# Low halves of eight weight pieces, the first block's sum and the first token mix made on TensorE, in a new order of steps

## The chip, the cores and the metric

The kernel runs on one core of a Trainium2 chip. The metric is the device time of one execution in microseconds (us); smaller is better. The kernel before takes 435.28 us (median of 3 runs, 435.2 to 435.55).

## What is computed

For 4 batches, 8 heads, 768 tokens and heads of 48 channels, a recurrence with a decaying state gives `x`, and a mixing network follows it:

```python
for t in range(S):
    y[:, :, t] = einsum('bhd,bhde->bhe', rt, state + (u * kt) vt)
    state = wt[..., None] * state + kt vt
x = y as (batch, seq, 384)
xt = x.transpose(0, 2, 1)
h = xt @ U @ V                      # U (768, 32), V (32, 768): a mix over tokens
u = x + h.transpose(0, 2, 1)
out = u + relu(u @ w_ch1) @ w_ch2   # 384 -> 1536 -> 384
```

`U`, `V`, `w_ch1` and `w_ch2` come as 64-bit floats, passed as pairs of 32-bit words.

## The kernel before, in words

**Chunks.** The recurrence is cut into 24 chunks of 128 tokens (6 for each batch; functions in `chunk(g)`). For a chunk VectorE makes two scans of the decays (step F, `scan_f`, and Q, `scan_q`; R between them takes reciprocals), and r and k are scaled by them (RP, KS: VectorE or GpSimd, "Pool"). TensorE makes scores (AM, `scores`), VectorE merges them under a mask into A (CP, `merge`), TensorE makes the output (YA from A and v, YZ from the state Z). The state goes from chunk to chunk: KT and KN turn k, DS multiplies it with v, ZM decays the sum (VectorE or ScalarE). The diagonal of A is a sum over channels of r, k and u: PR multiplies r and k, MD sums on TensorE (`rows_by_u`), DV copies, SEL and SEL2 spread it; chunks from 6 on use RK, RU and RED instead. XE brings the output to x (tile `xT`), XT and XN (or XD on VectorE) turn it for the token mix.

**Token mix and blocks.** `token_mix(b)` sums the six chunks of a batch against U (GA twice, G4, SELM; the high and low halves of the result by GS and GSL). The tokens are cut into 7 blocks of 384 or 512. For a block `make_u` multiplies the mix with V into PSUM (HP), adds it to x on VectorE (UADD), and splits the sum in a high half (UH) and a low half (UL), for each of three channel tiles. `ffn` then makes 12 groups UP of nine products each (high and low half of weights and of u), with relu halves HH and HL, and 12 groups DN of nine, the sum O and the store OUT. So block 0 can start only when all six chunks of batch 0 are through.

**Weights.** 27 pieces are loaded raw (LRAW) and converted (`split_raw`): E on ScalarE, C2 and C3 on VectorE (lines 302 and 315), ADD on GpSimd (line 322), the high half HI on ScalarE (line 332), and the low half SUB = value minus high half, on GpSimd or VectorE (line 339).

**Order.** Nothing is scheduled by a tool at build time: the table `ORDER` names each step in turn, three characters a step (its number, and whether it goes to its other engine, and how many warm-up products TensorE runs ahead of it, `lead`). Each engine runs its steps in the order of the table; SP issues all loads and stores in that order too. `plan` gives the buffers out in the same order: 3 PSUM buffers ("ffn") serve UP, DN, HP, XT, KT, MD and the mix; two buffers hold w, so the load LW of a chunk waits for Q of the chunk two before.

## Time and profile before

| | before |
|---|---|
| median of 3 runs | 435.28 us (435.2 to 435.55) |
| the profiled execution: span from first to last instruction | 433.5 us |
| around the span (median less span) | 1.8 us |
| TensorE busy, share of the span | 418.0 us, 96% |
| VectorE busy | 351.0 us, 81% |
| ScalarE, GpSimd busy | 185.5 us, 134.3 us |
| first product of a block (UP) | at 59.46 us |
| last product ends | at 427.97 us |

PE is TensorE, DVE VectorE, ACT ScalarE, POOL GpSimd, SPq the queue that issues the DMAs. A row of a timeline has the start in us, the duration, engine, line of the kernel, operation, the tile written and the tiles read, and how many equal instructions it merges. Products on TensorE overlap, so a row's cost to those behind it is the distance from its start to the next start. A matrix product on plain 32-bit floats shows two records each.

### The profile page before, as it was taken

What the parts mean: (1) busy time and instruction counts of PE and PEld (TensorE: products, weight loads), DVE (VectorE), ACT (ScalarE), POOL (GpSimd) and SP (SyncE); (2) the same over time, 40 slices, a digit from 0 to 9 for tenths busy, and PEclk for the clock granted to TensorE, in tenths of its full rate; (3) what the DMA queues carried; (4) which work ended last, traced back from release to release, by engine and by line L of the source; (5) the groups of instructions that cost most, each with busy time, mean ns of one, the idle gap of its engine ahead of it and who ended that gap; (6) DMA issues with size and microseconds to landing.
All of it is one profiled execution on the core that took longest, in us unless ns stands there. A gap on an engine that the chain in (4) does not pass through costs nothing. (4 is left out here: it accounts for less than half of the span.)

```text
span 433.5 us, 10486 instructions
## 1 busy us (share of the span) xinstructions
PE 418.0 (96%) x4156; PEld 363.0 (84%) x4156; DVE 351.0 (81%) x802; ACT 185.5 (43%) x527; POOL 134.3 (31%) x178
## 2 busy tenths in 40 slices
...
GB/s 279 327 267 338 204 132 310 110 198 172 272 80 217 123 242 158 23 26 107 98 64 231 119 23 117 81 119 122 8 30 74 1 162 39 36 104 206 2 2 60
DMA packets 23913, 57.29 MB, mean 132 GB/s; under 512 B 2864, under 2 KB 7856, under 8 KB 23856
## 3 DMA queue, kind: packets, MB, share of 16 engines
...
q8 instruction: 34, 0.56, 0.5%
...
## 5 line engine op out<-in xcount | busy, mean ns | idle before, releaser
L898 PE MATMUL f<-hid,w2h 128*128 128x384 f32 (+1 forms) x504 | 148.5, 364 | 0.0
L864 PE MATMUL f<-u,w1h 128*128 128x384 f32 (+1 forms) x504 | 147.8, 364 | 0.6 <-DVE xT L820 0.3
L864 PEld LDWEIGHTS f<-u,w1h 128*128 128x128 f32 x504 | 92.9, 188 | 12.9 <-issue 1.4
L898 PEld LDWEIGHTS f<-hid,w2h 128*128 128x128 f32 x504 | 92.9, 188 | 10.2 <-issue 0.7
L864 PE MATMUL f<-u,w1l 128*128 128x384 f32 (+1 forms) x252 | 90.8, 360 | 0.0
L898 PE MATMUL f<-hid,w2l 128*128 128x384 f32 (+1 forms) x252 | 90.7, 360 | 0.0
L869 ACT ACTIVATE hid<-f 128x384 fp32r<-128x384 f32 (+1 forms) x60 | 32.2, 538 | 96.9 <-PE f L864 88.9
L875 DVE SCALAR_TENSOR_TENSOR hid<-f,hid 128x384 fp32r<-128x384 f32 (+1 forms) x84 | 50.0, 608 | 11.2 <-ACT hid L869 10.5
L898 PEld LDWEIGHTS f<-hid,w2l 128*128 128x128 f32 x252 | 47.4, 188 | 4.7
L864 PEld LDWEIGHTS f<-u,w1l 128*128 128x128 f32 x252 | 47.4, 188 | 4.0
L679 DVE STREAM_TRANSPOSE kn<-rk 32x128 f32<-32x128 f32 x160 | 48.3, 302 | 2.5
L469 ACT ACTIVATE A<-ident,dv 128x128 f32<-128x128 f32 x140 | 43.8, 391 | 6.0 <-DVE dv L455 4.0
L916 DVE TENSOR_TENSOR xT<-f,xT 128x384 f32<-128x384 f32 (+1 forms) x21 | 12.7, 610 | 38.0 <-PE f L898 37.9
L831 POOL TENSOR_TENSOR u<-xT,u 128x512 fp32r<-128x512 f32 (+1 forms) x10 | 12.3, 1238 | 91.5 <-PE f L864 35.8
L322 POOL TENSOR_TENSOR cva_w<-cva_w,raw_w 128x384 int32<-128x384 int32 x24 | 25.0, 1055 | 41.1 <-DVE cva_w L315 15.7
L405 DVE TENSOR_TENSOR_SCAN Q<-w,starts,qd 128x258 f32<-128x258 f32 x48 | 33.3, 735 | 0.5 <-POOL rk L413 0.2
L551 DVE COPY_PREDICATED A<-maskf,aps 128x1024 f32<-128x1024 uint32 x24 | 31.6, 1315 | 0.4 <-PE aps L544 0.2
L390 DVE TENSOR_TENSOR_SCAN F<-w,qd 128x259 f32<-128x259 f32 x48 | 30.4, 675 | 0.5 <-DMA w<-in_wT 0.4
L716 DVE STREAM_TRANSPOSE xn<-xT 32x192 f32<-32x192 f32 x80 | 29.5, 369 | 1.1
L413 POOL TENSOR_TENSOR rk<-rk,Q 128x512 f32<-128x512 f32 x18 | 21.5, 1193 | 25.4 <-DVE Q L405 25.4
L871 DVE TENSOR_SCALAR hid<-f 128x384 fp32r<-128x384 f32 (+1 forms) x24 | 14.3, 596 | 17.7 <-PE f L864 14.4
L475 POOL TENSOR_SCALAR_AFFINE_SELECT A<-dv 128x128 f32<-128x128 f32 (+1 forms) x39 | 11.7, 333 | 43.1 <-DVE dv L455 20.0
...
## 6 DMA issues: line engine op xcount, KB each, us to landing
...
```

The source lines that it names most:

```text
L322: lambda: nc.gpsimd.tensor_tensor(out=d["to"].bitcast(I32), in0=d["a"].bitcast(I32), in1=d["e"], op=ALU.add),
L390: nc.vector.tensor_tensor_scan(out=back(F), data0=back(st["w"]), data1=back(qd, OVER * h), initial=1.0, op0=ALU.mult, op1=ALU.add)
L405: nc.vector.tensor_tensor_scan(out=st["Q"][:, a:e], data0=st["w"][:, a:e], data1=qd[:, a - OVER * h : e - OVER * h], initial=starts[:, h : ...
L413: ENG[eng].tensor_tensor(out=rk[:, 0], in0=rk[:, 0], in1=Qv, op=ALU.mult)
L469: nc.scalar.activation(to, one, AF.Copy, scale=dv[:, NP * i + j : NP * i + j + 1])
L551: nc.vector.copy_predicated(to, mask2, new)
L679: nc.vector.transpose(to[32 * j : 32 * j + 32, :, 32 * i : 32 * i + 32], src[32 * i : 32 * i + 32, :, 32 * j : 32 * j + 32])
L716: nc.vector.transpose(to[q, :, :, r], src[r, :, :, q])
L864: nc.tensor.matmul(ps, wt[:, f, ct, :], u[ct][:, z], start=(m == 0), stop=(m == 8))
L869: nc.scalar.activation(h[:, 0], d["ps", f], AF.Relu)
L875: nc.vector.scalar_tensor_tensor(out=h[:, 1], in0=d["ps", f], scalar=0.0, in1=h[:, 0].bitcast(F32), op0=ALU.max, op1=ALU.subtract)
L898: nc.tensor.matmul(d["o", ct], wt[:, 4 * ct + part, f - 3 * part, :], hid[f][:, z], start=(part == 0 and m == 0), stop=(part == 3 and m == 8),
```

## The change

With the lists `LOW_PE`, `X_PE`, `MIX_AT_ONCE` and `UP_PARTS`, and a new table:

- For w1 pieces 0 to 7 the SUB is replaced: TensorE adds the value times the identity and the high half times minus the identity in PSUM (LP, new lines 349 and 350), and ScalarE or VectorE copies the result out (LC). Six of the LC stand on ScalarE, two (w12, w15) on VectorE; a PSUM buffer is held meanwhile.
- Block 0: TensorE brings x into PSUM by the identity (XI) and adds HP to it there; UH and UL read the sum from PSUM, and ScalarE copies it back to x (UC). The three UADD go.
- Batch 0's mix: six steps GX sum one chunk each into one PSUM tile, in place of GA, G4 and SELM.
- UP of f = 0, 1, 2 in block 0 is cut into three steps UA by channel tile (the same nine products in another order).
- MD takes four products of 32 columns in place of one of 128.
- The order of all steps is new, as are the engines of those with two, and the warm-up products (14 before, 28 after).

First place, TensorE early on: MD 2 (`trd_267`), scores of chunk 1, YA 0, MD 3 (`trd_349`) and DS 0 before,

```order
L496 MATMUL trd_267<-u_diag,kr_225 128x2 x4
L544 MATMUL aps<-rk_175 64x128 x4
L544 MATMUL aps<-rk_175 64x64 x4
L544 MATMUL aps<-rk_175 64x128 x4
L544 MATMUL aps<-rk_175 64x64 x4
L622 MATMUL y_325<-A_195,v_193 32x128 x8
L632 MATMUL y_325<-A_195,v_193 32x128 x8
L496 MATMUL trd_349<-u_diag,kr_310 128x2 x4
L561 MATMUL dS<-v_193,kn_320 48x48 x8
```

and after the change (`trd_412` is MD 3, with the last of 9 warm-up products ahead of it, `lp_w` are LP w12 and LP w11):

```order
L200 MATMUL trd_412<-blank 128x384
L522 MATMUL trd_412<-u_diag,kr_408 32x2 x16
L572 MATMUL aps<-rk_214 64x128 x4
L572 MATMUL aps<-rk_214 64x64 x4
L572 MATMUL aps<-rk_214 64x128 x4
L572 MATMUL aps<-rk_214 64x64 x4
L349 MATMUL lp_w_480<-cva_w_2_282,ident 128x384
L350 MATMUL lp_w_480<-w1h,minus 128x384
L349 MATMUL lp_w_489<-cva_w_1_182,ident 128x384
L350 MATMUL lp_w_489<-w1h,minus 128x384
```

The scores of chunk 1 (AM 1) moved from ahead of MD 3 to behind it, and two LP stand behind them.

Second place, TensorE from the block's mix (HP) to the first product of block 0, before (`trk_1070` is KT 7, `trx_0_1114` XT 1.0),

```order
L815 MATMUL hp_2_1062<-Vst,gs_1003 128x384
L522 MATMUL trk_1070<-ident,rk_657 128x128 x4
L561 MATMUL dS<-v_930,kn_1022 48x48 x8
L544 MATMUL aps<-rk_657 64x128 x4
L544 MATMUL aps<-rk_657 64x64 x4
L544 MATMUL aps<-rk_657 64x128 x4
L544 MATMUL aps<-rk_657 64x64 x4
L735 MATMUL trx_0_1114<-ident,xT_1091 128x128 x3
L864 MATMUL f_0_3_1128<-u_0_1039,w1h 128x384
```

and after (YA 6 and HP 0.0 stand just ahead of these rows):

```order
L883 MATMUL hp_1_1180<-xT_438,ident 128x384
L865 MATMUL hp_1_1180<-Vst,gs_1113 128x384
L883 MATMUL hp_2_1186<-xT_438,ident 128x384
L865 MATMUL hp_2_1186<-Vst,gs_1113 128x384
L572 MATMUL aps<-rk_984 64x128 x4
L572 MATMUL aps<-rk_984 64x64 x4
L572 MATMUL aps<-rk_984 64x128 x4
L572 MATMUL aps<-rk_984 64x64 x4
L550 MATMUL trk_1220<-ident,rk_984 128x128 x4
L349 MATMUL lp_w_1225<-cva_w_7_1077,ident 128x384
L350 MATMUL lp_w_1225<-w1h,minus 128x384
L940 MATMUL f_0_3_1246<-u_0_1171,w1h 128x384
```

The two XI and LP w17 are new ahead of the first product; DS 6 went forward out of this stretch, and XT 1.0 behind the first eight groups.

Third place, VectorE from the merge of chunk 6 to the low halves of block 0, before (`gs` is GSL 0; the adds into `xT_436` are UADD),

```order
L551 COPY_PREDICATED A_921<-maskf,aps 128x1024
L781 TENSOR_TENSOR gs_1003<-gb_999,gs_1003 32x384
L390 SCALAR_TENSOR_TENSOR F_1014<-w_957,qd 128x259 x2
L820 TENSOR_TENSOR xT_436<-hp_0_1025,xT_436 128x384
L820 TENSOR_TENSOR xT_436<-hp_1_1037,xT_436 128x384
L820 TENSOR_TENSOR xT_436<-hp_2_1062,xT_436 128x384
L831 TENSOR_TENSOR u_0_1039<-xT_436,u_0_1039 128x384
```

and after:

```order
L579 COPY_PREDICATED A_967<-maskf,aps 128x1024
L809 TENSOR_TENSOR gs_1113<-gb_986,gs_1113 32x384
L479 TENSOR_REDUCE dv_1116<-kr_1052 128x8
L363 TENSOR_TENSOR w1l<-cva_w_8_1055,w1h 128x384
L308 TENSOR_SCALAR cva_w_9_1131<-raw_w_9_1127 128x384
L308 TENSOR_SCALAR cva_w_6_1133<-raw_w_6_1123 128x384
L321 SCALAR_TENSOR_TENSOR cva_w_9_1131<-raw_w_9_1127,cva_w_9_1131 128x384
L321 SCALAR_TENSOR_TENSOR cva_w_6_1133<-raw_w_6_1123,cva_w_6_1133 128x384
L887 TENSOR_TENSOR u_0_1171<-hp_0_1121,u_0_1171 128x384
```

F 8 and the three adds are out of this stretch; RED 7, SUB w18 and the conversions of w19 and w16 are in it.

The diff, with the table cut to a line:

```diff
--- before.py
+++ after.py
@@ -41,6 +41,10 @@
 BIG_BUFS, TURNING, CVA_BUFS, W_BUFS = 20, 4, 3, 2
 
 TURN_K_DVE, TURN_X_DVE = [12, 13, 14, 15, 16, 17, 18, 19, 20, 21, 22, 23], [12, 13, 14, 15, 16, 17, 18, 19, 20, 21, 22, 23]
+CHOICES = 3
+DIAG_PE, LATE_GUARD = [0, 1, 2, 3, 4, 5], []
+DIAG_V, MIX_AT_ONCE, X_PE, UP_PARTS = [], [0], [0], [0, 1, 2]
+LOW_PE = dict(w1=[0, 1, 2, 3, 4, 5, 6, 7], w2=[], V=[])
 ADD_Z_PE = (1, 2, 3, 4)
 W_MAX, W_MAX_BITS, DECAY_MIN = 1.25, 0x3FA00000, 1e-16
 HIGH_MIN, HIGH_END = 1.125 * 2.0**-15, 122880.0
@@ -60,46 +64,46 @@
 
 DIGITS = "0123456789ABCDEFGHIJKLMNOPQRSTUVWXYZabcdefghijklmnopqrstuvwxyz+-"
 ORDER = (
-    "2x02y02z03003203M03603713803303V03P03R03503N03C03W13413903U00J03Q12-03A13E03X03n03m03w03B10L03o00K03S00M04B0"
...
+    "3303800000203E03913A00300100403B03403F13D03C03U03d03X03Z00K00M03500L03G03H03I13J13V03e13c03f93u03Y13M03a03b1"
...
 )
 
 
@@ -137,9 +141,9 @@
         i, how = DIGITS.index(ORDER[n]) * 64 + DIGITS.index(ORDER[n + 1]), DIGITS.index(ORDER[n + 2])
         s = steps[i]
         assert s not in done and done.issuperset(s.after), s.name
-        if how % 2:
-            s.eng = s.alt
-        s.lead = how // 2
+        if how % CHOICES:
+            s.eng = s.alt[how % CHOICES - 1]
+        s.lead = how // CHOICES
         for buf in s.take:
             buf.slot = free[buf.pool].pop(0)
         for buf in s.bufs:
@@ -202,6 +206,8 @@
     warm(8, idle)
     ident = const.tile([P, P], F32, name="ident")
     make_identity(nc, ident)
+    minus = const.tile([P, P], F32R, name="minus")
+    nc.gpsimd.tensor_scalar(out=minus, in0=ident, scalar1=-1.0, scalar2=None, op0=ALU.mult)
     maskf = const.tile([P, NP, P], F32, name="maskf")
     nc.vector.memset(maskf, 1.0)
     for n, r, base in ((0, slice(0, P), 0), (NQ, slice(0, HP), -HP), (NQ, slice(HP, P), 0)):
@@ -241,7 +247,7 @@
 
     def step(name, eng, fn, after=(), take=(), use=(), alt=None):
 
-        s = Step(name, eng, fn, after, list(take), list(use), alt)
+        s = Step(name, eng, fn, after, list(take), list(use), alt.split() if alt else None)
         steps.append(s)
         return s
 
@@ -334,6 +340,24 @@
                 nc.vector.tensor_copy(d["hi"], d["a"])
 
         hi = step("HI " + nm, "ACT", high, [add], use=[bcva], alt="DVE")
+        if kind != "U" and i in LOW_PE[kind]:
+            blp = Buf("ffn")
+
+            def apart():
+                ps = d["lp"] = place("ffn", [P, TB], f"lp_{nm}", blp)
+                lead(ps)
+                nc.tensor.matmul(ps, ident, d["a"], start=True, stop=False)
+                nc.tensor.matmul(ps, minus, d["hi"], start=False, stop=True)
+
+            def rest(eng):
+                if eng == "ACT":
+                    nc.scalar.activation(d["lo"], d["lp"], AF.Copy)
+                else:
+                    nc.vector.tensor_copy(d["lo"], d["lp"])
+
+            lp = step("LP " + nm, "PE", apart, [hi], take=[blp], use=[bcva])
+            ready[key] = [hi, step("LC " + nm, "ACT", rest, [lp], use=[blp], alt="DVE")]
+            return
         sub = step(
             "SUB " + nm, "Pool",
             lambda eng: ENG[eng].tensor_tensor(out=d["lo"], in0=d["a_lo"], in1=d["hi_lo"].bitcast(F32), op=ALU.subtract),
@@ -352,7 +376,7 @@
         old = sts.get(g - 1) if c > 0 else None
         nm = str(g)
 
-        by_pe = g < 6
+        by_pe = g in DIAG_PE
 
         def load_w():
             st["w"] = place("w", [P, NP * SEG], f"w_{g}", buf["w"])
@@ -493,7 +517,11 @@
                 tr = st["trd"] = place("ffn", [P, NP, P], f"trd_{g}", btd)
                 lead(tr)
                 for j in range(NP):
-                    nc.tensor.matmul(tr[:, 0, j : j + NP + 1 : NP], st["kr"][:, j, :], u_diag[:, j, :], start=True, stop=True)
+                    for q in range(4):
+                        t = slice(32 * q, 32 * q + 32)
+                        nc.tensor.matmul(
+                            tr[t, 0, j : j + NP + 1 : NP], st["kr"][:, j, t], u_diag[:, j, :], start=True, stop=True
+                        )
 
             def copy_dv(eng):
                 st["dv"] = place("dv", [P, H], f"dv_{g}", buf["dv"])
@@ -780,6 +808,26 @@
             gs = d["gs"]
             nc.vector.tensor_tensor(out=gs[r], in0=d["gb"][r], in1=gs[r].bitcast(F32), op=ALU.subtract)
 
+        def at_once(c):
+            if c == 0:
+                d["gb"] = place("ffn", [P, DM], f"gb_{b}", bgb)
+                lead(d["gb"])
+            for m in range(3):
+                nc.tensor.matmul(
+                    d["gb"][RANK * m : RANK * (m + 1), :], U_sb[:, c, :],
+                    xns[b, c]["xn"].rearrange("p a b -> p (a b)"), start=(c == 0), stop=(c == NCH - 1),
+                )
+
+        if b in MIX_AT_ONCE:
+            gb = None
+            for c in range(NCH):
+                gb = step(
+                    f"GX {b}.{c}", "PE", lambda c=c: at_once(c), xns[b, c]["steps"] + ready.get(("U", 0), []) + [gb],
+                    take=[bgb] if c == 0 else [], use=[bgb, xns[b, c]["buf"]],
+                )
+            hi = step(f"GS {b}", "ACT", high, [gb], take=[d["buf"]], use=[bgb])
+            d["step"] = step(f"GSL {b}", "DVE", low, [hi], use=[bgb, d["buf"]])
+            return
         ga = [
             step(
                 f"GA {b}.{i}", "PE", lambda cs=cs: part(cs), [s for c in cs for s in xns[b, c]["steps"]] + ready.get(("U", 0), []),
@@ -798,7 +846,7 @@
     def make_u(blk, segs, xs):
 
         n = sum(w for _, _, w in segs)
-        d = ub[blk] = dict(n=n, bufs=[Buf("big") for _ in range(NCT)], uhs=[], uls=[], u={})
+        d = ub[blk] = dict(n=n, bufs=[Buf("big") for _ in range(NCT)], uhs=[], uls=[], u={}, kept={})
         bx = xbuf[blk]
         mixes = [gss[b] for b, _, _ in segs]
         vs = [s for i in range(2) for s in ready.get(("V", i), [])]
@@ -807,12 +855,14 @@
             bhp, bu = Buf("ffn"), d["bufs"][ct]
 
             def mix(ct=ct, bhp=bhp):
-                hp = d["hp", ct] = place("ffn", [P, n], f"hp_{blk}_{ct}", bhp)
-                lead(hp)
+                if blk not in X_PE:
+                    hp = d["hp", ct] = place("ffn", [P, n], f"hp_{blk}_{ct}", bhp)
+                    lead(hp)
+                hp = d["hp", ct]
                 cs = slice(ct * P, (ct + 1) * P)
                 at = 0
                 for b, t, w in segs:
-                    nc.tensor.matmul(hp[:, at : at + w], gss[b]["gs"][:, cs], Vst[:, t : t + w], start=True, stop=True)
+                    nc.tensor.matmul(hp[:, at : at + w], gss[b]["gs"][:, cs], Vst[:, t : t + w], start=blk not in X_PE, stop=True)
                     at += w
 
             def add(ct=ct):
@@ -821,10 +871,27 @@
 
             def high(eng, ct=ct, bu=bu):
                 u = d["u"][ct] = place("big", [P, 2, n], f"u_{blk}_{ct}", bu, dtype=F32R)
+                x = d["hp", ct] if blk in X_PE else blocks[blk][:, ct, 0:n]
                 if eng == "ACT":
-                    nc.scalar.activation(u[:, 0], blocks[blk][:, ct, 0:n], AF.Copy)
+                    nc.scalar.activation(u[:, 0], x, AF.Copy)
                 else:
-                    nc.vector.tensor_copy(u[:, 0], blocks[blk][:, ct, 0:n])
+                    nc.vector.tensor_copy(u[:, 0], x)
+
+            def first_x(ct=ct, bhp=bhp):
+                hp = d["hp", ct] = place("ffn", [P, n], f"hp_{blk}_{ct}", bhp)
+                lead(hp)
+                nc.tensor.matmul(hp, ident, blocks[blk][:, ct, 0:n], start=True, stop=False)
+
+            def low_of_sum(ct=ct):
+                u = d["u"][ct]
+                nc.vector.tensor_tensor(out=u[:, 1], in0=d["hp", ct], in1=u[:, 0].bitcast(F32), op=ALU.subtract)
+
+            def keep(eng, ct=ct):
+                x = blocks[blk][:, ct, 0:n]
+                if eng == "ACT":
+                    nc.scalar.activation(x, d["hp", ct], AF.Copy)
+                else:
+                    nc.vector.tensor_copy(x, d["hp", ct])
 
             def low(eng, ct=ct):
                 u = d["u"][ct]
@@ -833,9 +900,18 @@
                 )
 
             nm = f"{blk}.{ct}"
+            xi = [step("XI " + nm, "PE", first_x, xs[-1:], take=[bhp], use=[bhp, bx])] if blk in X_PE else []
             hp = step(
-                "HP " + nm, "PE", mix, [m["step"] for m in mixes] + [hp] + vs, take=[bhp], use=[m["buf"] for m in mixes],
+                "HP " + nm, "PE", mix, [m["step"] for m in mixes] + [hp] + vs + xi, take=[] if xi else [bhp],
+                use=[bhp] + [m["buf"] for m in mixes],
             )
+            if blk in X_PE:
+                uh = step("UH " + nm, "ACT", high, [hp] + ups[-1:], take=[bu], use=[bhp], alt="DVE")
+                d["uhs"].append(uh)
+                d["uls"].append(step("UL " + nm, "DVE", low_of_sum, [uh], use=[bhp, bu]))
+                d["kept"][ct] = [step("UC " + nm, "ACT", keep, [hp] + xs, use=[bhp, bx], alt="DVE")]
+                ups.append(uh)
+                continue
             ad = step("UADD " + nm, "DVE", add, [hp] + xs, use=[bhp, bx])
             uh = step(
                 "UH " + nm, "ACT", high, [ad] + ups[-1:], take=[bu], use=[bx], alt="DVE"
@@ -863,6 +939,16 @@
                 for m, (wt, ct, z) in enumerate(parts):
                     nc.tensor.matmul(ps, wt[:, f, ct, :], u[ct][:, z], start=(m == 0), stop=(m == 8))
 
+            def up_part(ct, f=f, bps=bps):
+                if ct == 0:
+                    ps = d["ps", f] = place("ffn", [P, n], f"f1_{blk}_{f}", bps)
+                    lead(ps)
+                u = d["u"][ct]
+                for wt, z in ((w1h, 0), (w1l, 0), (w1h, 1)):
+                    nc.tensor.matmul(
+                        d["ps", f], wt[:, f, ct, :], u[:, z], start=(ct == 0 and z == 0 and wt is w1h), stop=(ct == NCT - 1 and z == 1)
+                    )
+
             def high(eng, f=f, bh=bh):
                 h = hid[f] = place("big", [P, 2, n], f"hid_{blk}_{f}", bh, dtype=F32R)
                 if eng == "ACT":
@@ -876,7 +962,15 @@
                     out=h[:, 1], in0=d["ps", f], scalar=0.0, in1=h[:, 0].bitcast(F32), op0=ALU.max, op1=ALU.subtract
                 )
 
-            u = step(
+            if blk == 0 and f in UP_PARTS:
+                u = None
+                for ct in range(NCT):
+                    u = step(
+                        f"UA {nm}.{ct}", "PE", lambda ct=ct, go=up_part: go(ct), [d["uhs"][ct], d["uls"][ct], u] + ready.get(("w1", f), []),
+                        take=[bps] if ct == 0 else [], use=[bps, d["bufs"][ct]],
+                    )
+            else:
+              u = step(
                 "UP " + nm, "PE", up, d["uhs"] + d["uls"] + ready.get(("w1", f), []),
                 take=[bps], use=d["bufs"],
             )
@@ -918,8 +1012,8 @@
             def send(ct=ct):
                 nc.sync.dma_start(dst(ct), blocks[blk][:, ct, 0:n])
 
-            o = step(f"O {blk}.{ct}", "DVE", total, [prev], use=[bps, bx])
-            step(f"OUT {blk}.{ct}", "SP", send, [o], use=[bx])
+            o = step(f"O {blk}.{ct}", "DVE", total, [prev] + d["kept"].get(ct, []), use=[bps, bx])
+            dns.append(step(f"OUT {blk}.{ct}", "SP", send, [o], use=[bx]))
 
 
     def recurrence(xs):
@@ -1133,7 +1227,7 @@
     pc = step("PC", "PE", count, [pw], take=[bcnt])
     pd = step("PD", "DVE", decide, [pc], use=[bcnt])
     outs[NB - 1, NCT - 1][1].after.append(pd)
-    step("PF", "SP", fetch, [pd])
+    outs[NB - 1, NCT - 1][-1].after.append(step("PF", "SP", fetch, [pd]))
     with tc.manual_schedule():
         for s in plan(steps, caps):
             leading[0] = s.lead
```

## Rows read from the trace of the kernel before

**Rows 1.** Busy time by stage: us, PE, PEld, DVE, ACT, POOL, PEclk, DMA share, GB/s.

```profile
3.60:59.46 55.86, 50.78 (x895) 42.13 (x894) 54.75 (x115) 48.63 (x150) 32.76 (x37) 0.94 0.85 290
59.46:320.20 260.74, 259.07 (x2692) 221.66 (x2690) 250.97 (x587) 114.30 (x317) 97.54 (x129) 1.00 0.39 127
```

**Rows 2.** The chain of waits, two of its last steps: start, us, engine, tile, line.

```profile
320.85 0.58 PE ga L761 x8
...
427.97 0.56 DVE xT L916
```

**Rows 3.** What PE waited for from 59 us on: total us, times, longest.

```profile
PE ga L761 <- DVE xn L716: 1.0, 2, 0.7
PE gb L772 <- DVE xT L916: 0.7, 1, 0.7
PE hp L815 <- DVE xT L820: 0.7, 2, 0.5
PE gb L772 <- ACT g L767: 0.6, 1, 0.6
PE f L864 <- DVE xT L820: 0.3, 1, 0.3
PE f L864 <- DVE hid L875: 0.3, 1, 0.3
```

**Rows 4.** Timeline of PE up to the first product of block 0.

```profile
53.42 0.89 PE L772 MATMUL gb<-g,sel 128*96 128x384 f32 x2 [0.18 <-ACT g L767]
54.15 0.60 PE L522 MATMUL trk<-ident,rk 128*128 128x128 f32 x4
...
56.02 0.64 PE L622 MATMUL y<-A,v 128*32 128x128 f32 x16
...
57.03 0.45 PE L815 MATMUL hp<-Vst,gs 96*128 96x384 f32 x1
...
58.33 0.90 PE L544 MATMUL aps<-rk 48*64 48x128 f32 x32
59.16 0.55 PE L735 MATMUL trx<-ident,xT 128*128 128x128 f32 x3
59.46 0.42 PE L864 MATMUL f<-u,w1h 128*128 128x384 f32 x1
```

**Rows 5.** Timeline of DVE: a step F, 46.8 to 50 us, GSL 0.

```profile
23.36 1.24 DVE L390 TENSOR_TENSOR_SCAN F<-w,qd 128x259 f32<-128x259 f32 x2
...
46.82 1.01 DVE L339 TENSOR_TENSOR w1l<-cva_w,w1h 128x384 fp32r<-128x384 f32 x2
47.75 0.68 DVE L413 TENSOR_TENSOR rk<-rk,Q 128x512 f32<-128x512 f32 x1
48.35 0.42 DVE L418 TENSOR_TENSOR rk<-rk,F 128x256 f32<-128x256 f32 x1
...
49.02 0.62 DVE L302 TENSOR_SCALAR cva_w<-raw_w 128x384 uint32<-128x384 uint32 x2
49.56 0.55 DVE L315 SCALAR_TENSOR_TENSOR cva_w<-raw_w,cva_w 128x384 uint32<-128x384 uint32 x1
...
54.87 0.56 DVE L781 TENSOR_TENSOR gs<-gb,gs 32x384 fp32r<-32x384 f32 x1 [0.16 <-ACT gs L776]
```

**Rows 6.** Timeline of DVE, conversion of w11, and of POOL beside it.

```profile
9.28 0.85 DVE L302 TENSOR_SCALAR cva_w<-raw_w 128x384 uint32<-128x384 uint32 x1
...
11.35 0.87 DVE L315 SCALAR_TENSOR_TENSOR cva_w<-raw_w,cva_w 128x384 uint32<-128x384 uint32 x1
...
11.07 0.73 POOL L418 TENSOR_TENSOR kr<-rk 128x256 f32<-128x256 f32 x1 [0.41 <-DMA rk<-in_rkT]
```

**Rows 7.** Timeline of PE: warm-up and MD 2 early, MD 5 later.

```profile
1.26 3.60 PE L196 MATMUL idle<-blank 128*128 128x512 bf16 x8 [1.26 <-DVE blank L185]
...
12.69 1.71 PE L496 MATMUL trd<-u_diag,kr 128*128 128x2 f32 x8
...
35.47 0.95 PE L496 MATMUL trd<-u_diag,kr 128*128 128x2 f32 x8
```

78 lines of the change are left out of this document (39 added, 39 removed).

## The prediction

> **What bounds the kernel now.** I read four views, in this order.
>
> First the busy time by stage [rows 1]. From 3.6 to 59.46 us, where the recurrence runs up to the first product of block 0, VectorE is busy 54.75 of 55.86 us (98%), TensorE 50.78. So VectorE's queue sets the start; TensorE has some 5 us to spare, ScalarE 7. From 59.46 to 320.2 us TensorE is busy 259.07 of 260.74: there its work sets the pace, although VectorE (250.97) has little to spare.
>
> Second the chain of waits [rows 2]: it comes to TensorE at 320.85 us and stays there until the last product at 427.97; the last sum and store take it to the span's end, 433.5.
>
> Third, what TensorE waits for after 59 us [rows 3]: 3.6 us in all. Of these, 2.3 are waits for VectorE's adds, copies and low halves (1.0 + 0.7 + 0.3 + 0.3), 1.3 belong to the mixes' `gb` (0.7 for a free buffer, 0.6 for ScalarE).
>
> Fourth the timelines [rows 4 to 7], which give prices. A step's price is the distance from its start to the next start, since neighbours overlap.
>
> So: time = start of the first product + TensorE work behind it + TensorE's waits + tail. The profiled execution's own time is its span plus the 1.8 us around it, taken equal to the median, 435.28.
>
> **The start: VectorE's queue up to GSL 0.** Prices [rows 5]: SUB 0.47 (two take 46.82 to 47.75), RP 0.60, KS 0.67 and PR like it (the same two operations of 256 columns), C2 0.27, C3 0.47 (a duration of 0.55, less the overlap that a SUB shows). Step by step in the two orders, up to GSL 0:
> - gone: six SUB (2.8), two KS net (three go back to GpSimd, one comes; 1.3), one C2 with C3 (0.7): -4.8
> - added: three PR taken from GpSimd (2.0), one RP net (0.6), two LC, two ZM from ScalarE.
>
> No row of before shows LC, a copy of 384 columns out of PSUM. Below it stands C2 (0.27, one operand), above it C3 (0.55); GSL, 0.56 with both operands the same length, is no cheaper. I take 0.47, nearer to the rows that read PSUM: 0.9 for two (0.5 to 1.1). ZM, two operands of 384 columns, is priced as a SUB: 0.9. Sum +4.4. Net **-0.4** (ends: -0.8, -0.2). F 8 and the adds UADD stand behind GSL 0, so their removal does not count here. ScalarE gives up two ZM and gets four LC by then; it had 7 us free, so I cost that at nothing. The cover is VectorE's queue itself.
>
> **A new wait at CP 1.** AM 1 stood ahead of MD 3; now it stands behind it, and MD 3 needs PR 3, which VectorE makes itself. Between PR 3 and CP 1 VectorE has only a C3 (0.5) and F 5 (1.24 [rows 5]): 1.7 us. TensorE must in that time run MD 3 (0.95 at the later pace [rows 7]) and AM 1 (0.83, from 58.33 to 59.16 [rows 4]), with two handovers of some 0.16 (the wait shown at GSL [rows 5]): 2.1. **+0.4**, with everything behind CP 1 on VectorE, thus the whole start, waiting. Ends: 0, if the four products of 32 columns make MD shorter, and 2.8 more, as the clock rival works out.
>
> **VectorE beside GpSimd.** C2 and C3 of w11 took 0.85 and 0.87 us [rows 6], not 0.3 and 0.55; at 11.35 a GpSimd KS was running (from 11.07). I assume two such meetings again: 0. Ends: -0.8 (none) and the port rival's.
>
> **From GSL 0 to the first product.** Before: GSL ends at 55.43 [rows 5], the product starts at 59.46: 4.03. After: YA 6 begins when CP 6 ends, as GSL does, and takes 1.0 (56.02 to 57.03 [rows 4]), 0.4 of it behind GSL's end; three HP of 0.3 (0.45 [rows 4] less an overlap of some 0.15), 0.9; two XI (the third is through before) at the 0.73 of a `gb` step of two shorter-row products (53.42 to 54.15 [rows 4]), 1.4; AM 0.83; KT 0.5 (its 0.60 less such an overlap); LP w17 0.9 (one `gb` step plus 0.17 more, as its value product is plain 32-bit). Sum 5.0: **+1.0**. DS 6, which left this stretch, is in the 4.03 and not in the 5.0. The three UADD leave the path from HP to UH (about 0.5 each), but the first product waits in TensorE's own queue anyway, so that buys nothing. UP_PARTS likewise: UA 0.0 needs only the first UH, but its place in the queue is behind LP w17.
>
> First product: -0.4 + 0.4 + 1.0 = +1.0, at **60.5**.
>
> **TensorE's work behind it.** LP w16 (0.9) and XT 1.0 (0.3, 59.16 to 59.46 [rows 4]) have moved there: **+1.2**. The other seven LP, XI 0.0, GX and 14 more warm-ups lie before it, beside VectorE's queue, which covers them; without that cover seven LP alone would cost 6.3. The three groups cut in UA have the same nine products: 0.
>
> **TensorE's waits.** VectorE has, up to GSL 3, some 6.5 us less to do: about 13.5 go to other engines or into PSUM (7 HH, 4 SUB, 4 KS, 3 UADD, 3 RK, and smaller), 7 come (PR, LC, ZM, UH, CK); TensorE arrives later besides. So the waits for VectorE go, 2.3; the two at `gb` stay, since the steps around SELM 2 and 3 keep their order. **-2.3** (ends: 0 and -3.6).
>
> Sum: +1.0 + 1.2 - 2.3 = -0.1. Span 433.4, time **435.2 us**. That is inside 0.2% (0.87 us), about what a measurement of this kernel can tell from no change. This case's own range is 433.4 to 436.8: the ends of LC, of MD and half of those of the waits.
>
> **The rivals.**
>
> *Everything lands* (faster). MD with narrower products finishes in time, so no wait at CP 1 (-0.4); no C2 or C3 meets GpSimd (-0.8); the `gb` waits go too (-1.3): 432.7 us. For it: GpSimd loses three PR and many SUB; against it: KS and RP remain there in the same stretch.
>
> *TensorE starts at its lower clock* (slower). The clock column gives 0.94 for the stretch to 59.46 [rows 1], yet MD 2 takes 1.71 us at 12.69 and MD 5 only 0.95 at 35.47 [rows 7]: until past 20 us TensorE runs near the pace of its lower level, 1.2 of 2.4 GHz. Eleven more warm-ups of 384 columns (0.34 each, from 3.60 / 8 for 512 [rows 7]) stand in this stretch. If they do not change the clock, TensorE becomes the bound. I walk from 10.1 (MD 2's 12.69 less MD 1 and a KT at that pace, 1.7 and 0.9): MD 1 1.7, AM 0 1.5, KT 0 1.0, six warm-ups 2.0, KT 1 1.0, MD 2 1.7, five warm-ups 1.6, KT 2 1.0, that is 21.6; then, the pace doubling as it did before, YA 0 and DS 0 1.5, nine warm-ups 1.5, MD 3 and AM 1 1.8: 26.4. VectorE is at CP 1 at about 23.1 (an estimate: 3.6, where the stage begins, plus 19.5 us of its steps by the prices above, among them nine scan pairs of 1.24, CP as one): 3.3 late, 2.9 of it not yet counted, less 0.2 from waits behind: **437.9**. It decides as soon as TensorE is behind PR 3's end by more than the warm-ups ahead of MD 3. For it: the rows are that slow before. Against it: 14 more warm-ups keep TensorE busy in its holes. The Trainium skill (TensorE: Matmul & The Clock Gate, section "What's actually happening") says that the throttled state is the default and activity releases it; by that rule the warm-ups would bring the faster pace early and this rival falls. The early rows fit the first half of it (1.71 against 0.95); that warm-ups release it so early no row of before shows.
>
> *The shared port* (slower). Three PR move onto VectorE and three KS back to GpSimd, beside C2, C3 and RP. If every such meeting costs what w11's did (0.3 to 0.55, say 0.4 [rows 6]), nine of them cost 3.6 less the 0.8 already in before's time, and 0.6 of the rest falls into CP 1's wait: +2.2, **437.4**. The Trainium skill (SBUF — State Buffer, section "Who interferes with whom") has the rule: a VectorE instruction with two inputs in SBUF and a GpSimd one that reads SBUF lock each other out for a whole instruction. C3 at 11.35 agrees; PR beside GpSimd is in no row here, and most C2 and C3 of before run at full pace beside GpSimd.
>
> **How the numbers follow.** Forecast 0.46 (of it 0.11 over 0.2% faster, 0.25 within, 0.10 slower); everything lands 0.30; lower clock 0.16; port 0.08. Faster 0.30 + 0.11 = 0.41, same 0.25, slower 0.16 + 0.08 + 0.10 = 0.34. The range must reach into the first and second rivals: 432.2 (half a us under the first) to 438.0 leaves out less than 2 in 10.
>
> **What would show it.** First product at 60.5; a VectorE wait of about 0.4 us ahead of CP 1 (line 579) for `aps`; MD 1 and MD 2 at 1.7 or at 0.95 (clock); C2, C3, PR rows over 0.7 beside GpSimd (port); LP steps 0.9 apart; TensorE's waits behind the first product about 1.3 us, none on `xT`. I am wrong if the first product starts before 59.5 or behind 62, if the waits stay at 3.6, or if new waits of TensorE in block 0 (for HL, LC or PSUM buffers) exceed 1 us.

## The result, and the profile after

The changed kernel takes 440.18 us (median of 4 runs, 439.26 to 442.1) against 435.41 (4 runs, 435.2 to 435.65): ratio 1.0116, 95% interval 1.0088 to 1.0145. It is slower by about 5 us and lies above the range given. The profiled execution took 440.99 us with a span of 438.9. One execution of the kernel without LP, below, took 520.42 us at a granted clock of 0.75; its ratio and median are those of its three others.

The first product of block 0 starts at 65.30 us, not at 59.46 as before [rows 4] or at 60.5 as forecast. From it to the span's end it is 373.6 us, before 374.0. So the whole loss, 5.8 us, lies ahead of the first product, and 0.4 comes back behind it.

The busy times of a stretch show why (columns as in [rows 1]). Before, the last two stretches up to the first product:

```profile
40.00:47.65 7.65, 5.41 (x124) 4.62 (x124) 7.45 (x12) 6.16 (x19) 5.21 (x6) 0.78 0.66 237
47.65:59.46 11.81, 11.49 (x222) 8.47 (x219) 11.46 (x26) 10.64 (x29) 5.08 (x5) 1.00 0.74 254
```

After, from TensorE's last standstill on:

```profile
47.29:65.30 18.01, 18.01 (x241) 10.98 (x242) 14.59 (x30) 13.45 (x35) 7.41 (x9) 1.00 0.50 180
```

Before, TensorE's spare time lay ahead of 47.65 us (5.41 busy of 7.65 from 40 us on); in the last 11.8 us it was busy 11.49, as busy as VectorE, and only the six warm-up products, some 0.9 us from 54.58 on, could have made room. After, it works 18.01 of 18.01 us, while VectorE has 3.4 to spare. TensorE's queue has become the bound.

The same point of both programs is the end of chunk 4's YZ, at 47.65 us before and 45.66 after (timelines of PE, before, then after):

```profile
47.32 0.39 PE L649 MATMUL y<-rk,Z 128*32 128x128 f32 x8
...
54.58 1.14 PE L196 MATMUL hp<-blank 128*128 128x384 bf16 x6
...
45.33 0.40 PE L677 MATMUL y<-rk,Z 128*32 128x128 f32 x8
45.66 0.59 PE L349 MATMUL lp_w<-cva_w,ident 128*128 128x384 f32 x1
```

There the change is 2.0 us ahead. But from there to the first product TensorE needs 19.6 us and not 11.8. Read from the starts in the two timelines, the 7.8 us are about: five LP 4.9, a standstill ("hole") in LP w10 1.0, GX less GA and SELM 2.4, XI 1.9; less the warm-ups 0.9, some XT that stand earlier or later now 1.3, and idle time 0.3. What stands in TensorE's queue after (timeline of PE, some of its rows):

```profile
47.29 0.59 PE L349 MATMUL lp_w<-cva_w,ident 128*128 128x384 f32 x1 [1.04 <-issue]
...
56.55 1.49 PE L816 MATMUL gb<-xn,U_sb 128*32 128x384 f32 x12
57.97 0.91 PE L349 MATMUL lp_w<-cva_w,ident 128*128 128x384 f32 x2
58.42 0.63 PE L350 MATMUL lp_w<-w1h,minus 128*128 128x384 f32 x1
58.89 0.81 PE L883 MATMUL hp<-xT,ident 128*128 128x384 f32 x2
59.63 0.56 PE L589 MATMUL dS<-v,kn 128*48 128x48 f32 x16
60.12 0.64 PE L650 MATMUL y<-A,v 128*32 128x128 f32 x16
...
64.48 0.81 PE L349 MATMUL lp_w<-cva_w,ident 128*128 128x384 f32 x2
64.83 0.63 PE L350 MATMUL lp_w<-w1h,minus 128*128 128x384 f32 x1
65.30 0.33 PE L940 MATMUL f<-u,w1h 128*128 128x384 f32 x1
```

Five LP cost 0.8 to 1.0 us each there (57.97 to 58.89, 64.48 to 65.30; of w10's the part behind the hole, 0.6), 4.3 together; the six GX 4.3 (two in 56.55 to 57.97, 0.71 each); XI 0.55 to 0.74 (the first from its start to the next, the others as an XI with its HP, less the 0.28 of an HP before). Chunk 6's YA starts at 60.12, 3.3 us behind the end of CP 6 (56.87); before, it started 1.3 behind (56.02 [rows 4], CP 6 ending at 54.71). The two CP 6 (timelines of DVE, before, then after):

```profile
53.38 1.33 DVE L551 COPY_PREDICATED A<-maskf,aps 128x1024 f32<-128x1024 uint32 x1 [0.16 <-ACT g L767]
...
55.55 1.32 DVE L579 COPY_PREDICATED A<-maskf,aps 128x1024 f32<-128x1024 uint32 x1
```

VectorE's rows that took longer than before or waited (timeline of DVE after):

```profile
8.29 1.05 DVE L437 TENSOR_TENSOR rk<-rk,Q 128x512 f32<-128x512 f32 x1
...
15.30 1.04 DVE L321 SCALAR_TENSOR_TENSOR cva_w<-raw_w,cva_w 128x384 uint32<-128x384 uint32 x1
...
23.86 1.28 DVE L414 TENSOR_TENSOR_SCAN F<-w,qd 128x259 f32<-128x259 f32 x2 [0.60 <-ACT dv L529]
...
33.59 0.93 DVE L363 TENSOR_TENSOR Vst<-cva_V,Vst 32x384 fp32r<-32x384 f32 x1
...
47.92 0.36 DVE L308 TENSOR_SCALAR cva_w<-raw_w 128x384 uint32<-128x384 uint32 x1 [1.21 <-PE lp_w L349]
...
58.64 0.56 DVE L809 TENSOR_TENSOR gs<-gb,gs 32x384 fp32r<-32x384 f32 x1 [1.77 <-ACT gs L804]
```

The last two are waits for TensorE: C2 for the buffer that LP w10 has to release, GSL 0 for the last GX. TensorE's waits from 60 us on (columns as in [rows 3]) are 2.7 us after, 3.6 before:

```profile
PE hp L865 <- DVE xT L870: 0.7, 2, 0.5
PE gb L800 <- ACT g L795: 0.6, 1, 0.6
PE f L940 <- DVE hid L961: 0.6, 1, 0.6
PE ga L789 <- DVE xn L744: 0.3, 1, 0.3
PE y L650 <- DVE A L579: 0.3, 1, 0.3
PE hp L200 <- DVE xT L870: 0.2, 1, 0.2
```

### The profile page after: what moved, and what is told of

Same layout as the page of the kernel before. It is cut to its first block, busy times and chain, and to the rows that moved or that the text cites. A ratio compares the mean times of both kernels' runs of the same rounds, so it can differ in the third digit from the quotient of the medians.

```text
span 438.9 us, 10878 instructions
## 1 busy us (share of the span) xinstructions
PE 421.7 (96%) x4362; PEld 359.8 (82%) x4362; DVE 346.3 (79%) x783; ACT 185.1 (42%) x518; POOL 144.9 (33%) x196
## 4 chain that ended last, share of the span: by engine, by line
PE 46%; DVE 18%; issue 2%; ACT 0%; DVEq 0%
PE f L992 21%; PE f L940 20%; DVE kn L707 5%; DVE xn L744 3%; DVE hid L961 2%; DVE A L579 2%; DVE Q L429 2%; DVE F L414 1%; DVE dv L479 1%; PE y L650 1%; PE aps L572 1%; PE hp L865 1%; PE y L660 1%; DVE xT L870 1%; DVE Z L621 1%
## 5 line engine op out<-in xcount | busy, mean ns | idle before, releaser
L992 PE MATMUL f<-hid,w2h 128*128 128x384 f32 (+1 forms) x504 | 146.7, 363 | 0.0
L940 PE MATMUL f<-u,w1h 128*128 128x384 f32 (+1 forms) x486 | 141.2, 364 | 0.6 <-DVE hid L961 0.6
L940 PEld LDWEIGHTS f<-u,w1h 128*128 128x128 f32 x486 | 89.7, 188 | 11.0 <-DVE hid L961 1.1
L940 PE MATMUL f<-u,w1l 128*128 128x384 f32 (+1 forms) x243 | 87.8, 361 | 0.0
L955 ACT ACTIVATE hid<-f 128x384 fp32r<-128x384 f32 (+1 forms) x65 | 34.9, 542 | 99.1 <-PE f L940 95.4
L940 PEld LDWEIGHTS f<-u,w1l 128*128 128x128 f32 x243 | 45.7, 188 | 4.4
L493 ACT ACTIVATE A<-ident,dv 128x128 f32<-128x128 f32 x124 | 39.1, 395 | 6.1 <-DVE dv L479 6.0
L898 POOL TENSOR_TENSOR u<-xT,u 128x512 fp32r<-128x512 f32 (+1 forms) x12 | 14.7, 1235 | 62.2 <-issue 31.1
L1183 ACT ACTIVATE junk<-raw_w 128x384 uint8<-128x384 f32 x24 | 13.1, 545 | 41.4 <-DMA raw_w<-in_w 41.2
L499 POOL TENSOR_SCALAR_AFFINE_SELECT A<-dv 128x128 f32<-128x128 f32 (+1 forms) x51 | 15.2, 332 | 42.2 <-DVE dv L479 28.3
```

The source lines that it names most:

```text
L493: nc.scalar.activation(to, one, AF.Copy, scale=dv[:, NP * i + j : NP * i + j + 1])
L940: nc.tensor.matmul(ps, wt[:, f, ct, :], u[ct][:, z], start=(m == 0), stop=(m == 8))
L955: nc.scalar.activation(h[:, 0], d["ps", f], AF.Relu)
L992: nc.tensor.matmul(d["o", ct], wt[:, 4 * ct + part, f - 3 * part, :], hid[f][:, z], start=(part == 0 and m == 0), stop=(part == 3 and m == 8),
```

## The experiments

My theory behind the result, "queue" below: TensorE has no time to spare from 47 us on, so each product added there moves the first product. Its rivals: "code" (two holes of TensorE, 0.8 and 1.0 us, for which the trace shows no wait ("issue" in its rows), come from the many more instructions), "start" (the first loads and the first 40 us set it), and VectorE's queue. "Ratio" is to the kernel before, run beside; "first" is the first product in the profiled execution.

| kernel | ratio (95%) | first, us |
|---|---|---|
| the change | 1.0116 (1.0088 to 1.0145) | 65.30 |
| MD whole again | 1.0137 (1.0102 to 1.0173) | 65.69 |
| no LP | 1.0168 (1.0129 to 1.0207) | 67.16 |
| LP of w11, w12 alone kept | 1.0082 (1.0055 to 1.0108) | 62.42 |
| mix by GA, G4, SELM again | 1.0105 (1.0073 to 1.0136) | 65.39 |
| late LP, GX and XI taken back | 1.0174 (1.0142 to 1.0205) | 63.19 |
| UADD again | 1.0180 (1.0162 to 1.0198) | 67.65 |
| LP with one product | 1.0032 (1.0014 to 1.0051) | 63.80 |
| first loads as before | 1.0130 (1.0109 to 1.0151) | 65.73 |
| before, narrow MD alone | 1.0010 (0.9994 to 1.0025) | 58.60 |
| before, XI alone | 1.0068 (1.0046 to 1.0089) | 61.17 |
| before, eight LP alone | 1.0182 (1.0155 to 1.0209) | 67.46 |
| before, GX alone | 1.0074 (1.0047 to 1.0101) | 61.93 |
| before, LP of w11, w12 alone | 1.0072 (1.0048 to 1.0097) | 63.34 |
| MD in two products | 1.0091 (1.0068 to 1.0114) | 63.38 |
| MD in two, LP with one product | 1.0044 (1.0024 to 1.0063) | 61.17 |
| MD in two, two LP kept | 1.0077 (1.0060 to 1.0094) | 62.87 |
| before, three moves | 1.0001 (0.9991 to 1.0012) | 59.40 |
| before, three moves and w16 late | 1.0072 (1.0054 to 1.0090) | 59.23 |

### One part undone

MD whole:

```diff
-for q in range(4): matmul(tr[32 q : 32 q + 32, ...], kr[:, j, 32 q : 32 q + 32], ...)
+matmul(tr[:, ...], kr[:, j, :], ...)
```

> The changed kernel with MD as before, one product of 128 columns for each pair in place of four of 32; the order is the same. Queue theory (TensorE runs without a break from 47.3 us to the first product at 65.3, so its own work there sets the start): the six MD become about 0.5 us longer, but all six lie before 37.2 us, where TensorE still waits; first product within 0.5 of 65.3, time 439.3 to 441. Code theory (the two holes of TensorE for which the trace shows no wait, 0.8 us inside MD 5 and 1.0 inside LP w10, come from the many more instructions, MD's above all, and set the start): holes gone or moved, first product 1 to 2.5 us earlier, time 437.5 to 439.

441.58 us, first product at 65.69. The holes are gone but for 0.3 us, and nothing is gained: now TensorE runs at a granted clock of 0.83 from 33 to 43 us (windows), and YA takes 1.08 at 35.07 where the change has 0.64 at 33.37. The run is not clean: F 4 waits 1.57 us for its load, in the change 0.60. That wait is 0.2 to 1.6 us in the profiled executions of the changed kernel and its variants, and VectorE is late by as much.

```profile
33.00:43.00 10.00, 10.00 (x228) 8.52 (x227) 9.36 (x19) 7.68 (x26) 6.73 (x10) 0.83 0.68 228
```

All low halves as SUB, then all but w11 and w12 (the other six at the places of their LP):

```diff
-LP w1i (PE), LC w1i (ACT; DVE for w12, w15)
+SUB w1i (POOL; DVE for w12, w15)
```

> The changed kernel with all eight low halves as SUB again (six on GpSimd, w12 and w15 on VectorE), each at the place of its LP; nothing else moved. Queue theory: five LP between 45.6 us and the first product (0.85 us each, 4.2 in all) are off TensorE, and LP w16 (0.9) behind it: first product 3 to 4 us earlier, unless VectorE, which waited 1.8 us for the mix and 1.2 in the LP hole, binds first; time 435.5 to 437.5. Code theory: only the hole inside LP w10 goes, 1.0 to 1.6 us: time 438.5 to 439.2. Start theory (the later first load, u's diagonal and the meetings of VectorE with GpSimd up to 35 us set it): nothing before 45 us changes, time 440 or, with more GpSimd work beside VectorE, later.

> The changed kernel with LP for w11 and w12 alone (they run at 24.3 to 26.1 us); the six later ones are SUB again, at their places. Queue theory: within 0.5 us of the run without any LP, since early TensorE had time to spare, 435.5 to 437.5. If an LP costs by itself wherever it stands, 1.7 us slower than that run.

Without the late LP the first product comes 2.9 us earlier, at 62.42, close to what queue gives; of that 0.9 us stays in the median (439.3; 1.5 by the ratios), since TensorE then waits 1.0 us more in block 0 for VectorE's low halves. Without any LP it is 442.93, far worse, and the reason is none of my theories. SUB of w12 on VectorE, beside a run of GpSimd's KS (timelines of DVE, then POOL):

```profile
26.21 4.00 DVE L363 TENSOR_TENSOR w1l<-cva_w,w1h 128x384 fp32r<-128x384 f32 x1
...
26.22 0.68 POOL L442 TENSOR_TENSOR rk<-rk,F 128x256 f32<-128x256 f32 x1
26.86 0.68 POOL L444 TENSOR_TENSOR rk<-rk,F 128x256 f32<-128x256 f32 x1
27.50 0.68 POOL L442 TENSOR_TENSOR rk<-rk,F 128x256 f32<-128x256 f32 x1
28.15 0.68 POOL L444 TENSOR_TENSOR rk<-rk,F 128x256 f32<-128x256 f32 x1
28.78 1.01 POOL L363 TENSOR_TENSOR w1l<-cva_w,w1h 128x384 fp32r<-128x384 f32 x1
```

It takes 4.00 us, to 0.4 us behind the end of GpSimd's run at 29.79. In the change LC, one operand in PSUM, stands at the same place beside the same four KS (timeline of DVE after):

```profile
26.24 0.55 DVE L356 CAST w1l<-lp_w 128x384 fp32r<-128x384 f32 x1
```

So the early LP pays by keeping VectorE clear of GpSimd: 3.5 of the 4.7 us between the first products of the two runs.

The mix, then block 0's sum, as before:

```diff
-GX 0.0 ... GX 0.5;  XI 0.i, UC 0.i
+GA 0.0, GA 0.1, G4 0, RED 7, LP w14, SELM 0;  UADD 0.i behind HP 0.i
```

> The changed kernel with batch 0's mix by GA, G4 and SELM as before, in place of the six GX; LP w14 stands between GA and SELM. Queue theory: TensorE's work ahead of the first product is less by six GX (some 3.2 us) and more by GA and SELM (1.9): first product about 1.3 us earlier, and as YZ 5 no longer stands behind three GX, VectorE's wait of 1.8 us ahead of GSL 0 shrinks to under 1; time 438.5 to 439.5. Rival: the extra handover over ScalarE (G4) makes the mix later, first product 0 to 1 later, time 440 to 441.

> The changed kernel with block 0's sum by UADD on VectorE again, no XI and no UC. Queue theory: three XI (0.73 each, 2.2 us) leave TensorE's unbroken queue, all behind GX 0.5, and HP 0.2 no longer waits for its turn: first product 1.5 to 2.2 us earlier, 63.1 to 63.8, unless UADD, UH and UL (1.4 us of VectorE) come late: time 438 to 439.5. Rival (the path over the adds is what the change saves): no earlier, 440 or more.

The mix makes no difference that the intervals show: GSL's wait shrank to 0.8 us, but the holes grew from 1.8 us to 3.0, the buffer wait at LP from 1.2 to 1.9, and F 4's wait from 0.6 to 1.5, so this run can't price the mix. UADD costs 3.7 us more than XI in the medians (443.90 against 440.18; 2.8 by the ratios), where I expected a gain. In this order the adds stand behind four conversions in VectorE's queue (timeline of DVE):

```profile
62.09 1.02 DVE L321 SCALAR_TENSOR_TENSOR cva_w<-raw_w,cva_w 128x384 uint32<-128x384 uint32 x2
63.14 0.56 DVE L870 TENSOR_TENSOR xT<-hp,xT 128x384 f32<-128x384 f32 x1
64.35 1.01 DVE L898 TENSOR_TENSOR u<-xT,u 128x384 fp32r<-128x384 f32 x1 [0.65 <-ACT u L876]
```

HP was made by 62.7 us, its add starts at 63.14, and then each UADD, UH and UL waits for the one before. TensorE, which waits with them, is busy 2.21 of 4.65 us from 63.00 to 67.65, and behind that its granted clock is 0.50, the lower of its two levels (1.2 of 2.4 GHz):

```profile
67.65:71.00 3.35, 3.35 (x11) 3.35 (x12) 2.84 (x8) 3.35 (x9) 0.00 (x0) 0.50 0.03 7
```

In the change it is 1.00 there. So the wait costs some 1.7 us (half of 3.35) once more by the clock. Not all of the 4.8 us between the two profiled executions is UADD's, though: 1.4 lie ahead of 48.7 us, where both kernels do the same but this one's holes are longer, 1.0 between GSL 0 and the first product, 2.4 behind it. All three at once, and the loads:

```diff
-LP w10, w13 to w17; GX; XI
+SUB; GA, G4, RED 7, SELM; UADD
```

> The changed kernel with the six late low halves as SUB, the mix by GA, G4 and SELM, and block 0's sum by UADD again: what stays of the change is MD in four products, the two early LP, the first three products in parts, and the order of the steps. Queue theory: TensorE's added work ahead of the first product (LP 4.2, XI 2.2, GX less GA and SELM 1.3 us) is gone, so VectorE's queue sets the start: GSL 0 as in the run with early LP alone (57.2), first product 61 to 62; behind it VectorE, heavier by three adds, gives waits: time 436 to 439. If the order itself were good, 434.5 or less.

```diff
-LW 0, LRAW U0, LRK 0, LW 1, LRAW w11, LUD (SP)
+LW 0, LRK 0, LUD, LW 1, LRAW w11, LRK 1, LRAW U0 (SP); C2, C3, ADD of U0 behind PR 2
```

> The changed kernel with the first loads in the old order (w of chunk 0, r and k of chunk 0, u's diagonal, w of chunk 1, then the pieces; U behind r and k of chunk 1) and U's conversion some steps later on VectorE. Start theory: F 0 at 3.7 and PR 0 without a wait, the merges 0.5 to 0.7 us earlier and the first product as much: 439.5. Queue theory: TensorE's queue from 47 us depends on the merges too, so up to 0.7 earlier, no more; a gain of over 1.5 us would speak for the start.

Taking all three back gives 442.78, although the first product comes at 63.19, 2.1 us earlier than in the change. What is lost lies behind it, by the same UADD: TensorE waits 3.7 us for the adds and their UH (1.55, 1.10, 1.00), and its granted clock is 0.50 from 63.19 to 67.00 us and 0.75 from there to 75. So the new order is no good with UADD at this place; what the rest of it is worth, this run does not show. With the old loads CP 1 comes 0.8 us earlier (24.23, not 25.05), and the first product at 65.73 all the same. By CP 5 the lead is gone (43.69 against 43.62), 0.6 of it in holes that were longer: "start" finds no support, but a part of that size isn't ruled out.

### One part alone, on the kernel before

The same edits, each alone in the old order: LP and LC where SUB stood; XI ahead of HP, in place of the six warm-ups; GX where GA stood.

> The kernel before with one part of the change alone: MD as four products of 32 columns. Code theory (each 256 instructions of TensorE, weight loads counted, are one block of code, and TensorE stands still where a block has not come; MD now issues 64 instructions where it issued 16): holes without a shown wait appear ahead of 42 us, at a distance of 255 or 256 records from each other, time 436.5 to 438.5. Queue theory: MD ends 0.5 us sooner each and the start is VectorE's, time 434.8 to 435.6.

> The kernel before with block 0's sum alone made in PSUM (XI, UC; no UADD for block 0; XI 0.0 stands where the six warm-ups stood). Queue theory: three XI add 2.2 us to TensorE's queue behind GSL 0, of which the warm-ups' 0.9 were a wait: first product 0.8 to 1.3 us later; VectorE is three adds lighter, which takes 0.5 to 1.5 us of later waits: time 435.0 to 436.5. Rival (the sum over VectorE is what holds the first product, as undoing it in the changed kernel cost 3.7 us): first product earlier, time 433 to 434.5.

> The kernel before with the eight low halves alone moved to TensorE, each LP where its SUB stood, LC on the engine of the SUB or on ScalarE for GpSimd's. Queue theory: of the eight LP (0.85 us each) w11 and w12 stand early, where TensorE waits 4.7 us in all; the other six (5.1 us) stand where it is busy without a break, three of them or so behind the first product; VectorE and GpSimd gain nothing, as LC takes as long as SUB: time 438.5 to 441. Rival (TensorE has the 5 us to spare that its busy share up to 59 us shows, as the prediction took it): 435 to 436.5.

> The kernel before with batch 0's mix alone by six GX in place of GA, G4 and SELM, all six where GA stood. Queue theory: 3.2 us of GX against 1.9 of GA and SELM, and the handover over G4 (0.5 us and a wait of 0.2) gone; GSL 0 waits for it, so first product 0.3 to 1.0 us later: time 435.5 to 436.5. Rival: the shorter chain wins, 434.5 to 435.

> The kernel before with LP and LC for w11 and w12 alone, where their SUB stood (w12's LC on VectorE, w11's on ScalarE); the other six low halves stay SUB. If the place in TensorE's queue decides (early it waits 4.7 us in all, from 43 us on it does not), this costs 0 to 1.5 us of the 8.5 that all eight cost: time 435 to 436.5. If each LP costs alike wherever it stands (8.5 / 8 each, through the engines that wait for its copy), 2.1 us: 437.

Narrow MD is neutral (0.6 us of holes; the runs with XI alone and GX alone, with MD whole, have 0.8 and 0.6). By the ratios, of some 435 us, GX alone costs 3.2 us, XI alone 3.0, LP alone 7.9, two early LP alone 3.1. Each is dearer than the products that it adds to TensorE, since engines work in order and wait for each other. GX: 36 records in one piece put AM 6 behind them, and CP 6 waits (PE, then DVE):

```profile
50.94 4.07 PE L812 MATMUL gb<-xn,U_sb 128*32 128x384 f32 x36
...
55.98 1.31 DVE L575 COPY_PREDICATED A<-maskf,aps 128x1024 f32<-128x1024 uint32 x1 [2.38 <-PE aps L568]
```

LP: w11's copy stands in ScalarE's queue until TensorE is through MD 3 and DS 0, and w13's in VectorE's (ACT, then DVE, of the run with all eight):

```profile
22.16 0.49 ACT L354 ACTIVATE w1l<-lp_w 128x384 fp32r<-128x384 f32 x1 [4.04 <-PE lp_w L350]
...
52.61 0.56 DVE L356 CAST w1l<-lp_w 128x384 fp32r<-128x384 f32 x1 [2.18 <-PE lp_w L350]
```

So my expectation that an early LP costs little, TensorE having time there, was wrong for the old order: the two cost 1.6 us each. TensorE was also slower there: LP w11's products took 1.65 and 1.09 us at 20.21, w12's 0.91 and 0.63 at 30.72. XI: TensorE waits 0.96 for a buffer that UC must release, and VectorE 1.47 for UH.

### TensorE's time alone, and the holes

```diff
-matmul(ps, ident, d["a"], start=True, stop=False)
-matmul(ps, minus, d["hi"], start=False, stop=True)
+matmul(ps, minus, d["hi"], start=True, stop=True)
```

> The changed kernel whose LP leaves out its first product (the value times the identity), so that LC copies minus the high half; each engine keeps all its other instructions. That takes TensorE 0.5 to 0.6 us from each LP and nothing from any other engine. Queue theory: five LP between 45.6 us and the first product give 2.5 to 3 us, the first product at 62.3 to 62.8, and 0.5 more behind it: time 436.5 to 438. Code theory: the hole stays if instructions are late at that place, first product 65 or so. VectorE theory (its queue sets GSL 0): under 1 us.

437.58 us, 2.6 less in the medians and 3.7 by the ratios, with no other engine's instruction touched: a clear run for queue, but for the holes, which it also moves (2.3 us of them, 1.8 in the change). The first product came 1.5 us earlier in the profiled execution, which with 440.34 was the slowest of six (436.1 to 440.3).

```diff
-for q in range(4): t = slice(32 * q, 32 * q + 32)
+for q in range(2): t = slice(64 * q, 64 * q + 64)
```

> The changed kernel with MD as two products of 64 columns, 32 instructions with their weight loads where the change has 64 and before 16. Code theory: the holes in TensorE stand at other instructions, still 255 or 256 records apart, and smaller or gone ahead of 42 us; first product 0.5 to 2 us earlier if the clock holds (columns of granted clock at 1.00 up to 47 us), 438 to 439.8. If the clock drops as with MD whole (granted 0.5 to 0.9 somewhere between 30 and 43 us), no gain: 440 to 441.6.

> The changed kernel with MD as two products of 64 columns and each LP without its first product (the value times the identity is left out; LC copies minus the high half). If the code holes and TensorE's own queue are two separate parts of the loss, the gains of the two runs add, 1.1 and 2.6 us: time 436.0 to 437.0, first product at 61.5 to 62.5. If they are one and the same (the queue is late only because of the holes), 437.5 to 438.5.

> The changed kernel with MD as two products of 64 columns and the six late low halves as SUB at the places of their LP. If both parts add here too (1.1 and 0.9 us): 437.8 to 438.6, first product at 60.5 to 61.5; the waits of TensorE in block 0 for VectorE stay as in the run with early LP alone (1.0 for a low half of the hidden values). Rival: VectorE's queue holds the first product at 62.4 as there, 439.

The holes follow the count of instructions. In the kernel with UADD, whose first 48 us are those of the change, they stand at the last five records of MD 5, the last of YZ 3 and the second of LP w10 (timeline of PE):

```profile
37.60 0.23 PE L522 MATMUL trd<-u_diag,kr 128*32 128x2 f32 x5 [1.09 <-issue]
42.11 0.27 PE L677 MATMUL y<-rk,Z 128*32 128x128 f32 x1 [0.28 <-issue]
48.67 0.59 PE L349 MATMUL lp_w<-cva_w,ident 128*128 128x384 f32 x1 [1.59 <-issue]
```

Counting records from one to the next (windows; products, then weight loads, in brackets):

```profile
37.55:42.08 4.53, 4.23 (x127) 3.46 (x128) 4.50 (x10) 3.29 (x14) 3.89 (x6) 1.00 0.62 187
42.08:48.64 6.56, 4.98 (x128) 3.89 (x127) 4.54 (x10) 4.68 (x13) 3.10 (x4) 1.00 0.97 322
```

127 + 128 = 255 both times, and the holes stand at the same instructions in the runs with GA and with the old loads. In the run with LP of one product, which issues fewer ahead of the place, the hole has slid to the last two records of MD 5. With MD in two products, half of its records, the holes are gone (0.2 us) and, unlike with MD whole, the clock stays at 1.00 in this stretch (it was 0.68 from 10 to 22 us):

```profile
30.00:43.00 13.00, 12.64 (x361) 10.40 (x360) 12.91 (x27) 11.36 (x39) 7.88 (x11) 1.00 0.79 255
```

The first product comes 1.9 us earlier (63.38) and the median falls by 1.1, within the overlap of the intervals. But it does not add to the other gains: with cheap LP 437.18 against 437.58, with two LP kept 439.08 against 439.3, all within their scatter. Whether holes and queue are two parts or one stays open.

The same pair shows the queue by itself. MD in two products and MD in two with cheap LP differ by one product of each LP alone, and the longest hole in either is 0.23 us. With cheap LP the first product comes at 61.17, not 63.38, though CP 5 was 0.8 us later, and the time falls by 1.9 us (439.08 to 437.18, 2.0 by the ratios, whose intervals do not meet). So TensorE's added products cost time where no hole has a part in it.

### A better order?

```diff
-DS 4, XT 0.2 (PE); GUARD 6, ZM 3 (ACT); SUB w15, SUB w18 (DVE)
+XT 0.2, DS 4 (PE); ZM 3, GUARD 6 (ACT); SUB w15, SUB w18 (POOL)
-C2 w16, C3 w16 ahead of CP 6 (DVE; second kernel only)
+C2 w16, C3 w16 behind UL 0.2
```

> Nothing of the change: the kernel before with three moves in its order. XT 0.2 goes ahead of DS 4 into TensorE's longest wait (2.4 us), ZM 3 ahead of GUARD 6 on ScalarE, which ends that wait 0.9 us sooner, and SUB of w18 and w15 from VectorE to GpSimd (0.47 us each off VectorE's queue ahead of GSL 0). If VectorE's and TensorE's queues bound the start together, as the runs of the changed kernel say, both must become shorter for a gain: the first product 0.5 to 1.0 us earlier, time 434.2 to 434.8. If GpSimd's two SUB hold up VectorE (0.4 us a meeting), 435 to 435.6.

> As the run with three moves, and C2 and C3 of w16 behind block 0's low halves (0.74 us more off VectorE's queue ahead of GSL 0, used only for the tenth group of block 0). First product 0.5 us earlier still if VectorE is the later of the two queues, time 433.7 to 434.4; if TensorE's own chain (XT 0.3 to 0.5, GA, SELM) is the later, no more than the three moves give.

The three moves gain nothing (first product at 59.40). VectorE lost two SUB (0.94 us), but beside GpSimd's SUB and KS the next SUB, RP and half a KS take 0.78, 1.08 and 1.17 us from 46.44 on, 1.6 beyond their prices, as the rival had it. The second kernel starts at 59.23 and loses it and more to one wait of TensorE in block 0, while VectorE itself had waited 1.9 us for a buffer of a SUB on GpSimd:

```profile
PE f L864 <- DVE hid L875: 2.6, 2, 2.4
```

No kernel run here beats the one before beyond its interval.

## Why the prediction was wrong, step by step

**The cover.** The step that failed is "TensorE has some 5 us to spare" and, from it, "the other seven LP, XI 0.0, GX and 14 more warm-ups lie before it, beside VectorE's queue, which covers them". The 5 us were an average over [rows 1]'s 56 us; in the last 11.8 of them TensorE had 0.3, and 0.9 of warm-ups. From the end of YZ 4 on it needed 7.8 us more than before, and of the work above only LP w17 and two XI were in the sum. The runs with cheap LP show what such work costs: 1.9 us without holes, 2.6 with them, for 0.5 to 0.6 us off each LP. My warning ("without that cover seven LP alone would cost 6.3") had the price and the wrong odds. The rival that should have stood there, TensorE's own queue at full clock, was missing.

**The forecast's 60.5 against 65.30**, 4.8 us, falls into three. Up to CP 6: forecast level, measured +2.2 (55.55 against 53.38). VectorE's listed waits up to there grew from 0.8 to 3.2 us, 1.2 of it at LP w10's hole, 0.7 at the first loads, 0.6 at F 4 (the trace names ScalarE's DV; F also waits for its load, to which most other runs put the same wait). At GSL 0: forecast as before (0.16), measured 1.77, +1.6. From GSL 0's end to the first product: forecast 5.0, measured 6.1, +1.1: the rest of XI 0.0 (0.4 us), DS 6 (0.5) and all of YA 6 (1.0, where 0.4 was forecast) were still to come, and the rest took 0.4 less than its prices. The wait of 0.4 at CP 1 did not come: the narrow MD 3 took 0.36 us (23.13 to 23.49), where the sum had 0.95, AM 1 was through by 24.4, and CP 1 started when F 4 was done (the prediction calls it F 5).

**VectorE's work** came out about right: -0.4 forecast, some -0.3 measured (2.2 later with 2.4 more of waits), meetings with GpSimd included. From start to next start LC took 0.46 and 0.47 us, ZM 0.45 and 0.47: the 0.47 taken for each was right.

**The sum in PSUM**, "that buys nothing", held for the old order, where this part alone costs 3.0 us, and not for the new one, where undoing it costs 2.8 to 3.7 (some of that by longer holes and by the clock). The path HP, UADD, UH, UL was priced by what TensorE's queue hid before; the new order had moved conversions ahead of it.

**TensorE's waits behind**: forecast 1.3, measured 2.7, of which 2.1 still for VectorE. Net behind the first product -1.1 forecast, -0.4 measured; the +1.2 of LP w16 and XT 1.0 went in as forecast, and some 0.7 on the good side is unaccounted for.

**The rivals.** The lower clock did not decide: after the early warm-ups KT 2 took 0.60 at 18.59 and AM 1 0.90 at 23.49 (timeline of PE after), though AM 0 still took 1.56. Before, two KT still took 1.97 at 20.29. MD 2's 0.44 is no measure of the clock, since its products have another shape now; and the column of the granted clock reads 1.00 from 10 to 22 us in both kernels, so the pace is read from the rows.

```profile
12.10 1.56 PE L572 MATMUL aps<-rk 48*64 48x128 f32 x32
...
17.40 0.44 PE L522 MATMUL trd<-u_diag,kr 128*32 128x2 f32 x32
...
18.59 0.60 PE L550 MATMUL trk<-ident,rk 128*128 128x128 f32 x4
...
23.49 0.90 PE L572 MATMUL aps<-rk 48*64 48x128 f32 x32
```

The Trainium skill's rule (TensorE: Matmul & The Clock Gate, "What's actually happening") that activity releases the throttle agrees with these rows. The port rival was right in kind and half in size: four long meetings by 51.5 us (1.05, 1.04 and 0.93 above, and a KS of 0.73 at 50.87), about 1.7 us beyond normal, against 0.8 in before's two, and they lie inside the -0.3. The longest meeting, 4.00 us, was seen only in the run without LP.
